# Loading one row of W2 in five few-engine transfers between the K/V loads, and moving the loads of x, gate and biases

## The chip, the cores and the metric

The kernel runs on one core of a Trainium2 chip. The metric is the device time of one execution in microseconds (us), median over runs. Before the change it is 364.52 us over 3 runs (364.5 to 364.59).

## What is computed

A decode step for 8 sequences mixes two branches with a learned gate. Cut to what matters (all tensors bfloat16; B = 8, D = 576, 32 query heads, 16 K/V heads of 128, cache length 8192, window W = 2048, F = 4608):

```python
def reference(A_x, A_k_cache, A_v_cache, A_wq, A_wo, B_x, B_w1, B_b1, B_w2, B_b2, gate_w):
    x = A_x
    g = _sigmoid((x * gate_w).sum(-1, keepdims=True))
    # attention over the last W = 2048 positions of the caches
    q = (x @ wq).reshape(B, Sq, Hq, Dh).transpose(0, 2, 1, 3)
    k = jnp.repeat(k_cache[:, :, Sk - W:, :], rep, axis=1)
    v = jnp.repeat(v_cache[:, :, Sk - W:, :], rep, axis=1)
    p = _softmax(jnp.einsum("bhqd,bhkd->bhqk", q, k) * (Dh ** -0.5))
    o = jnp.einsum("bhqk,bhkd->bhqd", p, v)
    a = o.transpose(0, 2, 1, 3).reshape(B, Sq, Hq * Dh) @ wo
    # two-layer MLP on the normalised input
    y = _layernorm(x)
    h = _gelu(jnp.einsum("bsd,df->bsf", y, w1) + b1)
    b = jnp.einsum("bsf,fd->bsd", h, w2) + b2
    return g * a + (1 - g) * b
```

Almost all of the work is reading: 32 blocks of 4 MB from the two caches and about 20 MB of weights. Each number that is read is used once or a few times.

## The kernel before

**Who issues what.** Every load is issued by SyncE (SP) on one queue; the 16 DMA engines of the core share the transfers of that queue. The kernel is written as a list of operations with dependences (`deps`, which become semaphore waits) and bare order (`after`). A planner (`_Plan.schedule`) with a cost for each operation turns the list into one fixed order per engine. The order on SP is chained by hand: each load has `after=last_dma[-1:]`, so it keeps the order of the text below.

**The first loads (L407 to L417).** In this order: the last 64 rows of Wq (`d_wqr`), the other 512 rows (`d_wqm`, 4 MB), x (`d_x`, 8 rows of 1152 bytes), the gate weights (`d_gw`, one row of 1152 bytes), b1 (`d_b1`, 4 rows of 2304 bytes), b2 (`d_b2`, one row of 1152 bytes), then W1 in two loads (`d_w1m`, 4.5 MB, and `d_w1r`). x starts the prologue: transposes of x on TensorE (L430), the gate (L440 to L458), the layer norm (L446 to L453), q (`o_qp`, L515), the selection of q's heads (`o_selp`, L530), the first MLP product (`o_hp`, L551), GELU and the transpose of h (`o_hT`, L562). b2 enters through a small accumulating product `m2_b` (L856), placed right after `o_hp`.

**The stream (L586 to L618).** 16 units of K and 16 of V follow, 4 MB each, as K0, K1, V0, K2, V1, K3 and so on. Four slots hold them in turn; a load waits on SP until the slot's last reader is done (`slot_free`). For each unit VectorE transposes K (`tr`, L718), TensorE multiplies q by it (`qk`, L732), VectorE takes a maximum (L645), ScalarE the exponential (L649), and TensorE multiplies by V (`pv`, L755 with the helper at L188).

**The end.** W2 has 4608 rows, laid on 128 partitions with 36 rows each, so "column j" is one row for each partition: 128 pieces of 1152 bytes, 41,472 bytes apart in memory. After the last V come 24 columns of W2 (`M` 0), Wo in two loads (`W` 0 and 1), and the last 12 columns of W2 as three loads of 8, 3 and 1 columns (`M` 1), from

```python
        M_CUTS = [[24], [8, 3, 1]]
        stream += [("M", 0), ("W", 0), ("W", 1), ("M", 1)]
```

All their products are added up in one bank of PSUM by `AccGroup` (L570 to L583, matmul at L579). Then VectorE and ScalarE copy one half each (L900 and L901) and SP stores the output (L903).

Of the kernel before, what the change touches and what calls it, by code (L numbers as in the profile page):

```python
# [191 lines left out]
        tile_size=(128, 128), tile_position=(0, 0)))  # L192


def build_kernel(nc, A_x, A_k_cache, A_v_cache, A_wq, A_wo, B_x, B_w1, B_b1, B_w2, B_b2, gate_w, out):
    B, Sq, D = A_x.shape
    _, Hkv, Sk, Dh = A_k_cache.shape
# [27 lines left out]
    with ExitStack() as es:  # L225
# [74 lines left out]
        def aoffs(name):  # L300
            return R[name][0] // 2
# [71 lines left out]
        OC = 64  # L373

        eng_sems = {e: es.enter_context(nc.semaphore("sem_" + e)) for e in ENGS}
        dma_keys = ["x", "g", "b", "b2", "wq", "w1", "out"] + ["s%d" % i for i in range(ND + 1)] + ["t%d" % i for i in range(5)]
        dma_sems = {k: es.enter_context(nc.semaphore("dma_" + k)) for k in dma_keys}

        P = _Plan()
# [28 lines left out]
        d_wqm = dma("sp", lambda e: e.dma_start(wq_m.rearrange("p t c -> p (t c)"), A_wq[0:512, :].rearrange("(p t) c -> p (t c)", t=4)), "wq", 512 * 8192, name="d_wqm", after=[d_wqr])  # L408
        dwq = [d_wqm, d_wqr]
        d_x = dma("sp", lambda e: e.dma_start(x_sb, x2), "x", 8 * D * 2, name="d_x", after=[d_wqm])  # L410
        d_gw = dma("sp", lambda e: e.dma_start(gw_sb, gate_w.partition_broadcast(1)), "g", D * 2, name="d_gw", after=[d_x])
        d_b1 = dma("sp", lambda e: e.dma_start(b1c, B_b1.rearrange("(c f) -> c f", c=FC)), "b", F * 2, name="d_b1", after=[d_gw])
        d_b2 = dma("sp", lambda e: e.dma_start(b2_sb, B_b2.partition_broadcast(1)), "b2", D * 2, name="d_b2", after=[d_b1])
        dx = [d_x]
        db = [d_b1]
        d_w1m = dma("sp", lambda e: e.dma_start(w1_m.rearrange("p t c -> p (t c)"), B_w1[0:512, :].rearrange("(p t) c -> p (t c)", t=4)), "w1", 512 * F * 2, name="d_w1m", after=[d_b2])
        d_w1r = dma("sp", lambda e: e.dma_start(w1_r, B_w1[512:576, :].rearrange("k (s c) -> (k s) c", s=2)), "w1", 64 * F * 2, name="d_w1r", after=[d_w1m])  # L417
        dw1 = [d_w1m, d_w1r]


# [167 lines left out]
        for vi in range(NU):  # L588
# [252 lines left out]
            if i == 0:  # L841
                filler("fill", 8, o_m2[-1:])

        o_m2, o_bias = [], []

        def filler(name, n, after):
            def fn(e):
# [5 lines left out]
            o_m2.append(add("pe", fn, deps=[exp_done[NU - 1], o_mrow, o_mcol], name=name, cost=0.21 * n, after=after))  # L853

        def bias(i):
            o_bias.append(AccGroup("m2_b", [(ob[:, 0:8], b2_sb), (ob[:, 8:16], b2_sb)], [d_b2, o_obl, o_obh], cost=0.6, after=[o_hp]).op)  # L856

        def m2_chunk(ci):
            s = take_slot()
            j = sum(sum(c) for c in M_CUTS[:ci])  # L860
            at = 0
            src = B_w2.rearrange("(p j) n -> p (j n)", j=FT)
            ops = []
            for n, jn in enumerate(M_CUTS[ci]):
                d = dma("sp", (lambda j=j, jn=jn, at=at: lambda e: e.dma_start(slot(s)[:, at * D:(at + jn) * D], src[:, j * D:(j + jn) * D]))(),
                        "t%d" % (sum(len(c) for c in M_CUTS[:ci]) + n), 128 * jn * D * 2, deps=slot_free[s] if n == 0 else [], name="d_w2_%d_%d" % (ci, n), after=last_dma[-1:])
                last_dma.append(d)
                mms = [(hT[:, j + k, 0:8], slot(s)[:, (at + k) * D:(at + k + 1) * D]) for k in range(jn)]
# [4 lines left out]
            slot_free[s] = ops  # L873

        query(0)
# [81 lines left out]
```

## Time and profile before

| what | value |
|---|---|
| median of 3 runs | 364.52 us (364.5 to 364.59) |
| profiled execution, span | 363.0 us |
| what lies around the span (364.52 - 363.0) | 1.5 us |
| mean granted TensorE clock | 0.958 |
| DMA: bytes, mean rate | 154.45 MB, 426 GB/s |
| PE / DVE / ACT / POOL busy | 82% / 64% / 46% / 6% |

The span goes from the first to the last instruction of the core. The busy shares are averages over the whole span. In the answers of the trace "DMA share" is the mean busy share of the 16 DMA engines in a stretch of time; a transfer's packet counts in the stretch in which it starts, so that a stretch shorter than a packet can show more than 1. "us to landing" runs from the issue on SP to the last completion, with the time in the queue.

### The profile page before, as it was taken

How to read it: one execution, taken by the hardware profiler on the slowest of the kernel's cores; microseconds unless marked ns; L12 is line 12 of the kernel's file. 1: busy time of each engine (PE TensorE's matmuls, PEld its weight loads, DVE VectorE, ACT ScalarE, POOL GpSimd, SP SyncE). 2: the span in 40 equal slices, each digit the busy share in tenths (PEclk: the TensorE clock that was granted, in tenths of full speed). 3: DMA queues.
4: the chain of work that ended last, by engine and by line, in shares of the span. 5: the costliest groups of instructions: out<-in, count | busy, mean ns of one | idle time of the engine just before them, and what ended most of it. 6: DMA issues, size and time to landing. Idle time of an engine off the chain costs nothing.

```text
span 363.0 us, 4821 instructions
## 1 busy us (share of the span) xinstructions
PE 297.9 (82%) x1954; PEld 125.3 (35%) x1423; DVE 231.4 (64%) x166; ACT 168.6 (46%) x130; POOL 22.9 (6%) x52
## 2 busy tenths in 40 slices
PE   0456366999999979998897979997989698999875
PEld 0111000434252615242433417150615152436742
DVE  0452989576666694929385768566675949295720
ACT  1022106656647463663637373838374554656000
POOL 9032030000010000000100000000000000003000
PEclk9976598999999998999999989999999999999999
DMA  8999999999999999999999999999999999999996
GB/s 347 436 437 406 455 412 455 412 455 412 450 415 451 415 451 413 441 426 441 426 441 426 435 430 437 430 437 428 437 430 437 430 435 430 437 430 433 415 430 257
DMA packets 6102, 154.45 MB, mean 426 GB/s; under 512 B 694, under 2 KB 840, under 8 KB 1228
## 3 DMA queue, kind: packets, MB, share of 16 engines
q1 hardware_dynamic: 6092, 154.30, 98.8%
q8 instruction: 8, 0.13, 0.1%
q14 instruction: 2, 0.02, 0.0%
HBM read 154.29 MB, written 0.01 MB: 425 GB/s over the span
## 4 chain that ended last, share of the span: by engine, by line
DMA 56%; DVE 27%; PE 14%; issue 1%; ACT 1%; SPq 0%; POOL 0%
DMA arena<-in_A_k_cache_dram 47%; DVE arena L718 21%; PE ps L175 6%; DMA arena<-in_B_w_dram 6%; DMA arena<-in_A_x_dram 3%; DVE arena L668 2%; PE ps L188 2%; PE ps L755 2%; PE ps L732 2%; DVE arena L645 1%; PE ps L501 0%; PE ps L579 0%; DVE arena L557 0%; DVE arena L521 0%; ACT arena L536 0%
## 5 line engine op out<-in xcount | busy, mean ns | idle before, releaser
L718 DVE STREAM_TRANSPOSE arena<-arena 128x4096 f32<-128x4096 f32 (+1 forms) x34 | 141.7, 4175 | 21.9 <-DMA arena<-in_A_k_cache_dram 21.9
L674 ACT ACTIVATE arena<-arena 32x2048 bf16<-32x2048 bf16 x60 | 114.5, 1908 | 71.4 <-DVE arena L668 42.9
L175 PE MATMUL ps<-arena 128*128 128x512 bf16 (+3 forms) x531 | 136.1, 402 | 0.0
L188 PE MATMUL ps<-arena 128*128 x840 | 109.5, 277 | 7.3 <-issue 1.2
L188 PEld LDWEIGHTS ps<-arena 128*128 x840 | 81.4, 97 | 34.3 <-issue 19.0
L732 PE MATMUL ps<-arena 128*128 128x512 bf16 x128 | 51.4, 401 | 27.6 <-DVE arena L718 26.1
L645 DVE TENSOR_REDUCE arena<-ps 128x1 f32<-128x2048 f32 x16 | 36.7, 2291 | 53.8 <-PE ps L175 53.8
L732 PEld LDWEIGHTS ps<-arena 128*128 128x128 bf16 x128 | 12.5, 98 | 131.7 <-issue 75.3
L649 ACT ACTIVATE arena<-ps,arena 128x2048 bf16<-128x2048 f32 x16 | 40.7, 2543 | 0.5
L646 ACT ACTIVATE arena<-arena 128x1 f32<-128x1 f32 x16 | 3.2, 203 | 63.5 <-DVE arena L645 63.5
L755 PE MATMUL ps<-arena 128*128 128x256 bf16 x184 | 25.3, 272 | 1.1 <-DVE arena L663 1.1
L755 PEld LDWEIGHTS ps<-arena 128*128 128x128 bf16 x184 | 16.9, 99 | 18.8 <-issue 14.6
L668 DVE STREAM_TRANSPOSE arena<-arena 128x1024 f32<-128x1024 f32 x15 | 18.1, 1205 | 2.9 <-ACT arena L649 2.9
L579 PE MATMUL ps<-arena 128*8 128x288 bf16 (+1 forms) x140 | 9.6, 286 | 4.0 <-DMA arena<-in_A_wo_dram 3.3
L739 POOL MEMSET arena<- 128x4096 f32 x1 | 3.5, 3511 | 148.2 <-PE ps L175 148.2
L685 PE MATMUL ps<-arena 128*128 128x512 bf16 x16 | 6.5, 407 | 6.5 <-ACT arena L649 5.2
L629 POOL COPY arena<-arena 32x64 bf16<-32x64 bf16 x16 | 3.7, 229 | 123.3 <-PE ps L175 122.4
L901 ACT ACTIVATE arena<-ps 8x288 bf16<-8x288 f32 x1 | 0.4, 402 | 19.5 <-PE ps L579 19.5
L422 DVE COPY arena<-arena 8x128 bf16<-8x128 bf16 x2 | 0.5, 228 | 13.9 <-DMA arena<-in_A_x_dram 13.9
L579 PEld LDWEIGHTS ps<-arena 128*8 128x8 bf16 (+1 forms) x140 | 5.8, 86 | 9.9 <-DMA arena<-in_A_wo_dram 3.3
L900 DVE CAST arena<-ps 8x288 bf16<-8x288 f32 x1 | 0.4, 446 | 12.3 <-PE ps L579 12.3
L557 DVE TENSOR_TENSOR arena<-arena 128x1152 f32<-128x1152 f32 x1 | 1.4, 1358 | 9.7 <-ACT arena L555 9.7
(106 smaller groups left out, 94.0 us busy)
## 6 DMA issues: line engine op xcount, KB each, us to landing
arena<-in_A_k_cache_dram SPq DMA_DIRECT2D x16, 4096.0 KB, 28.7
arena<-in_A_v_cache_dram SPq DMA_DIRECT2D x16, 4096.0 KB, 25.5
arena<-in_B_w_dram SPq DMA_DIRECT2D x1, 4608.0 KB, 22.0
arena<-in_A_wo_dram SPq DMA_DIRECT2D x2, 2304.0 KB, 23.8
arena<-in_A_wq_dram SPq DMA_DIRECT2D x1, 4096.0 KB, 12.6
arena<-in_B_w_dram SPq DMA_DIRECT2D x1, 3456.0 KB, 24.1
arena<-in_B_w_dram SPq DMA_DIRECT2D x1, 1152.0 KB, 22.3
arena<-in_B_w_dram SPq DMA_DIRECT2D x1, 576.0 KB, 23.0
```

Of the source, the lines that this page charges most:

```text
L175: return e.add_instruction(mybir.InstMatmult(name=nc.get_next_instruction_name(), engine=mybir.EngineType.PE, ins=[e.lower_ap(rhs), e.lowe ...
L188: return e.add_instruction(mybir.InstMatmult(name=nc.get_next_instruction_name(), engine=mybir.EngineType.PE, ins=[rhs, lhsT], outs=[e.low ...
L579: ins = e.matmul(ps[32 * j:32 * j + 8, BK_ACC, 0:JN], lhsT, rhs[:, JN * j:JN * j + JN], start=False, stop=True, skip_group_check=True, til ...
L629: return e.tensor_copy(dst, src)
L645: mx = add("dve", lambda e: e.tensor_reduce(out=k(g, MX + x), in_=scores, axis=AXL.X, op=ALU.max), deps=[qk_unit[t]], name="mx%d" % t, cos ...
L649: ex = add("act", lambda e: e.activation(out=bass.AP(arena, offset=aoffs("P"), ap=[[AST, 128], [64, 32], [1, 2], [2, 32]]), in_=ps[:, 0:4, ...
L668: pc = add("dve", lambda e: e.transpose(view("PC").bitcast(F32), view("P").bitcast(F32)), deps=[ex] + (sp_done[t - 1][0] if t else [o_acc0 ...
L674: return e.activation(out=bass.AP(arena, offset=32 * a * AST + aoffs(home) + 64 * a, ap=[[AST, 32], [256, 32], [1, 64]]), in_=bass.AP(aren ...
L685: mm = e.matmul(*args, start=True, stop=False, skip_group_check=True) if n == 0 else held_matmul(nc, e, *args, start=True, stop=False, ski ...
L718: return e.transpose(bass.AP(arena_f, offset=foffs(base) + 2048 * h0, ap=[[AST // 2, 128], [1, 2048 * nh]]), bass.AP(arena_f, offset=foffs ...
L732: mm = e.matmul(*args, start=False, stop=True, skip_group_check=True) if rc == 0 else held_matmul(nc, e, *args, stop=True, skip=True)
L755: return e.matmul(dst, bass.AP(arena, offset=aoffs(home) + 256 * q + ee, ap=[[AST, 128], [2, 128]]), slot(s).rearrange("p (r k d) -> p r k ...
```

## The change

It has three parts.

1. **Order of the first loads.** x comes between the two loads of Wq, the gate weights between Wq and W1, b1 between the two loads of W1, and b2 between K0 and K1. `m2_b` now waits for that later b2.
2. **One column of W2 out of the end.** The last three loads of W2 are 7, 3 and 1 columns instead of 8, 3 and 1. The last column (128 rows of 1152 bytes) goes to a place of its own, `w2x`, which is laid over the constants `sel` and `sel4` once `o_selp` and `o_hp` have read them. A small product `m2_x` uses it.
3. **How that column is read.** Five loads, put into the stream behind K3, K4, K5, K6 and K7, each read as n groups of m rows: 16 x 1, 11 x 3, 5 x 13, 3 x 4 and 2 x 1. The destination has n x m partitions, the source an outer dimension of n. They are built by a new helper that takes both patterns as they are written.

```diff
+def grouped_read(nc, e, dst, src):
+    return e.add_instruction(mybir.InstDMACopy(
+        name=nc.get_next_instruction_name(), engine=mybir.EngineType.SP, queue="qSPDynamicHW", mode="Copy",
+        ins=e.lower_ap_dma(src), outs=e.lower_ap_dma(dst), oob_is_err=True, cce_op=ALU.bypass))
...
-        req("sel", 4 * 128, BF)
-        req("sel4", 128, BF)
+        req("selb", 5 * 128, BF)
...
+        over("sel", "selb", 0, 4 * 128, BF)
+        over("sel4", "selb", 1024, 128, BF)
+        over("w2x", "selb", 0, D, BF)
...
-        d_wqm = dma("sp", ..., name="d_wqm", after=[d_wqr])
+        d_x = dma("sp", ..., name="d_x", after=[d_wqr])
+        d_wqm = dma("sp", ..., name="d_wqm", after=[d_x])
-        d_x = dma("sp", ..., name="d_x", after=[d_wqm])
-        d_gw = dma("sp", ..., name="d_gw", after=[d_x])
-        d_b1 = dma("sp", ..., name="d_b1", after=[d_gw])
-        d_b2 = dma("sp", ..., name="d_b2", after=[d_b1])
+        d_gw = dma("sp", ..., name="d_gw", after=[d_wqm])
+        d_w1m = dma("sp", ..., name="d_w1m", after=[d_gw])
+        d_b1 = dma("sp", ..., name="d_b1", after=[d_w1m])
+        d_w1r = dma("sp", ..., name="d_w1r", after=[d_b1])
-        d_w1m = dma("sp", ..., name="d_w1m", after=[d_b2])
-        d_w1r = dma("sp", ..., name="d_w1r", after=[d_w1m])
...
-        M_CUTS = [[24], [8, 3, 1]]
+        M_CUTS = [[24], [7, 3, 1]]
...
         def m2_chunk(ci):
...
+            if ci == 0:
+                o_m2.append(AccGroup("m2_x", [(hT[:, FT - 1, 0:8], w2x)], [o_hT, d_w2x[-1]], cost=0.2, prio=-1, after=o_m2[-1:]).op)
...
+        w2x = view("w2x")
+        X_PARTS = [(16, 1), (11, 3), (5, 13), (3, 4), (2, 1)]
+        d_w2x = []
+
+        def bias_row(i):
+            d_b2.append(dma("sp", lambda e: e.dma_start(b2_sb, B_b2.partition_broadcast(1)), "b2", D * 2, name="d_b2", after=last_dma[-1:]))
+            last_dma.append(d_b2[0])
+            bias(0)
+
+        def row_part(i):
+            n, m = X_PARTS[i]
+            p0 = sum(a * b for a, b in X_PARTS[:i])
+            dst = bass.AP(arena, offset=p0 * AST + aoffs("w2x"), ap=[[AST, n * m], [1, 1], [1, D]])
+            src = B_w2.rearrange("(p j) n -> p (j n)", j=FT)[p0:p0 + n * m, (FT - 1) * D:FT * D].rearrange("(n m) c -> n m c", n=n)
+            d_w2x.append(dma("sp", lambda e: grouped_read(nc, e, dst, src), "w2x", n * m * D * 2, deps=[o_selp, o_hp] if i == 0 else [], name="d_w2x%d" % i, after=last_dma[-1:]))
+            last_dma.append(d_w2x[-1])
+
+        stream.insert(1, ("B", 0))
+        for i in range(len(X_PARTS)):
+            stream.insert(7 + 3 * i, ("R", i))
...
-        bias(0)
         for kind, i in stream:
-            {"K": k_item, "V": v_item, "W": wo_chunk, "M": m2_chunk, "B": bias}[kind](i)
+            {"K": k_item, "V": v_item, "W": wo_chunk, "M": m2_chunk, "B": bias_row, "R": row_part}[kind](i)
```

When the changed kernel is built, the planner puts `m2_x` on TensorE between the two halves of the QK products of K7; `m2_b` stays right behind `o_hp`; on GpSimd two small copies for the head selection move ahead of eight others. The order of everything else on each engine's long stretch is that of before.

More of the change, by code (lines that the diff above doesn't have):

```diff
@@ L375, in build_kernel @@
         eng_sems = {e: es.enter_context(nc.semaphore("sem_" + e)) for e in ENGS}
-        dma_keys = ["x", "g", "b", "b2", "wq", "w1", "out"] + ["s%d" % i for i in range(ND + 1)] + ["t%d" % i for i in range(5)]
+        dma_keys = ["x", "g", "b", "b2", "wq", "w1", "w2x", "out"] + ["s%d" % i for i in range(ND + 1)] + ["t%d" % i for i in range(5)]
         dma_sems = {k: es.enter_context(nc.semaphore("dma_" + k)) for k in dma_keys}
@@ L407, in build_kernel @@
         d_wqr = dma("sp", lambda e: e.dma_start(wq_r, A_wq[512:576, :].rearrange("k (s c) -> (k s) c", s=2)), "wq", 64 * 8192, name="d_wqr")
[L408 removed]
+        d_x = dma("sp", lambda e: e.dma_start(x_sb, x2), "x", 8 * D * 2, name="d_x", after=[d_wqr])
+        d_wqm = dma("sp", lambda e: e.dma_start(wq_m.rearrange("p t c -> p (t c)"), A_wq[0:512, :].rearrange("(p t) c -> p (t c)", t=4)), "wq", 512 * 8192, name="d_wqm", after=[d_x])
         dwq = [d_wqm, d_wqr]
[L410 to L413, printed above, removed]
+        d_gw = dma("sp", lambda e: e.dma_start(gw_sb, gate_w.partition_broadcast(1)), "g", D * 2, name="d_gw", after=[d_wqm])
+        d_w1m = dma("sp", lambda e: e.dma_start(w1_m.rearrange("p t c -> p (t c)"), B_w1[0:512, :].rearrange("(p t) c -> p (t c)", t=4)), "w1", 512 * F * 2, name="d_w1m", after=[d_gw])
+        d_b1 = dma("sp", lambda e: e.dma_start(b1c, B_b1.rearrange("(c f) -> c f", c=FC)), "b", F * 2, name="d_b1", after=[d_w1m])
+        d_w1r = dma("sp", lambda e: e.dma_start(w1_r, B_w1[512:576, :].rearrange("k (s c) -> (k s) c", s=2)), "w1", 64 * F * 2, name="d_w1r", after=[d_b1])
         dx = [d_x]
         db = [d_b1]
[L416 to L417 removed]
         dw1 = [d_w1m, d_w1r]
@@ L855, in bias @@
         def bias(i):
-            o_bias.append(AccGroup("m2_b", [(ob[:, 0:8], b2_sb), (ob[:, 8:16], b2_sb)], [d_b2, o_obl, o_obh], cost=0.6, after=[o_hp]).op)
+            o_bias.append(AccGroup("m2_b", [(ob[:, 0:8], b2_sb), (ob[:, 8:16], b2_sb)], [d_b2[0], o_obl, o_obh], cost=0.6, after=[o_hp]).op)
         def m2_chunk(ci):
@@ L873, in m2_chunk @@
             slot_free[s] = ops
+        w2x = view("w2x")
[12 more added lines that the diff above has]
+            last_dma.append(d_w2x[-1])
+        assert sum(a * b for a, b in X_PARTS) == 128
+        stream.insert(1, ("B", 0))
+        for i in range(len(X_PARTS)):
+            stream.insert(7 + 3 * i, ("R", i))
         query(0)
-        bias(0)
         for kind, i in stream:
-            {"K": k_item, "V": v_item, "W": wo_chunk, "M": m2_chunk, "B": bias}[kind](i)
+            {"K": k_item, "V": v_item, "W": wo_chunk, "M": m2_chunk, "B": bias_row, "R": row_part}[kind](i)
         seq = []
```

2 lines of the change are left out of this document (1 added, 1 removed).

## The prediction

> **What bounds the kernel now.** I read the page first (DMA line, DMA queues, chain), then the windows of DMA share, then the timeline of the last microseconds. The page:
>
> ```profile
> span 363.0 us, 4821 instructions
> ...
> DMA  8999999999999999999999999999999999999996
> ...
> DMA packets 6102, 154.45 MB, mean 426 GB/s; under 512 B 694, under 2 KB 840, under 8 KB 1228
> ...
> q8 instruction: 8, 0.13, 0.1%
> ...
> DMA 56%; DVE 27%; PE 14%; issue 1%; ACT 1%; SPq 0%; POOL 0%
> ```
>
> The DMA engines are busy in every slice but the first and the last. The chain has DVE and PE pieces too, but the windows say that they only run beside a full queue:
>
> ```profile
> 36.00:100.00 64.00, 50.48 (x260) 15.59 (x162) 50.17 (x18) 30.88 (x22) 3.51 (x1) 0.89 1.00 434
> 100.00:200.00 100.00, 90.88 (x560) 39.12 (x409) 68.45 (x44) 55.72 (x41) 1.84 (x8) 0.98 1.00 432
> 200.00:300.00 100.00, 87.00 (x554) 38.23 (x403) 68.52 (x46) 54.26 (x40) 0.00 (x0) 0.98 1.00 432
> ```
>
> The last two numbers are DMA share and GB/s: share 1.00 and 432 to 434 GB/s from 36 to 300 us, with no hole. So the time is a short start, the bytes at this rate, and what follows the last byte. Each of the 16 engines moves 432 / 16 = 27 bytes per ns. The change moves the same bytes, so it can only alter how evenly the engines end, what small loads cost them, and the start. The end, first by DMA share, then by instructions:
>
> ```profile
> 357.00:358.60 1.60, 1.60 (x30) 1.10 (x24) 0.00 (x0) 0.00 (x0) 0.00 (x0) 1.00 0.97 405
> 358.60:359.00 0.40, 0.17 (x4) 0.00 (x0) 0.00 (x0) 0.00 (x0) 0.00 (x0) 1.00 0.72 279
> 359.00:359.20 0.20, 0.00 (x0) 0.00 (x0) 0.00 (x0) 0.00 (x0) 0.00 (x0) 1.00 0.80 317
> 359.20:359.40 0.20, 0.02 (x2) 0.02 (x4) 0.00 (x0) 0.00 (x0) 0.00 (x0) 1.00 0.59 230
> 359.40:359.60 0.20, 0.20 (x4) 0.16 (x6) 0.00 (x0) 0.00 (x0) 0.00 (x0) 1.00 0.67 271
> 359.60:359.80 0.20, 0.20 (x8) 0.14 (x4) 0.00 (x0) 0.00 (x0) 0.00 (x0) 1.00 0.41 161
> 359.80:360.00 0.20, 0.20 (x8) 0.14 (x5) 0.00 (x0) 0.00 (x0) 0.00 (x0) 1.00 0.53 196
> 360.00:360.20 0.20, 0.20 (x8) 0.17 (x4) 0.00 (x0) 0.00 (x0) 0.00 (x0) 1.00 0.46 161
> 360.20:360.40 0.20, 0.20 (x6) 0.01 (x2) 0.00 (x0) 0.00 (x0) 0.00 (x0) 1.00 0.22 75
> 360.40:360.60 0.20, 0.20 (x8) 0.15 (x6) 0.00 (x0) 0.00 (x0) 0.00 (x0) 1.00 0.00 0
> ```
>
> ```profile
> 360.42 0.22 PEld L579 LDWEIGHTS ps<-arena 128*8 128x8 bf16 x6 [0.21 <-DMA arena<-in_B_w_dram]
> 360.79 0.09 PEld L579 LDWEIGHTS ps<-arena 128*8 128x8 bf16 x2 [0.15 <-DMA arena<-in_B_w_dram]
> 361.12 0.40 ACT L901 ACTIVATE arena<-ps 8x288 bf16<-8x288 f32 x1 [19.48 <-PE ps L579]
> ...
> 361.61 0.32 SPq L903 DMA_DIRECT2D out_dram<-arena  x1
> ```
>
> The engines do not end together. From 358.6 to 360.4 the idle part is 0.4 x 0.28 + 0.2 x (0.20 + 0.41 + 0.33 + 0.59 + 0.47 + 0.54 + 0.78) = 0.11 + 0.66 = 0.78 us per engine. At 360.0 to 360.2 still 0.46 x 16 = 7.4 engines move data, and half of the engines have ended up to 1.5 us before. TensorE waits for the last of them (360.79), and from there to the end stand 363.0 - 360.79 = 2.2 us that the change leaves alone. So 0.78 us, 0.21% of 364.52, is the most that any redistribution of the same bytes can gain.
>
> The q8 line fits a late half: eight code packets, 0.13 MB / 8 = 16 KB each, 0.1% of 16 x 363 us = 5.8 us in all, 0.7 us each (0.4 to 1.1 with the rounding), at the cost of the engine that carries one. The Trainium skill (Runtime: NRT & Kernel Launch, Instruction fetch mechanics) says that crossing a 16 KB block of code is "mostly hidden". The size agrees with this trace, but a full DMA queue hides nothing from the engine that carries the block.
>
> **The first loads.** Pieces of the chain in order of time, then SP's issues in the timeline:
>
> ```profile
> 1.71 12.15 DMA arena<-in_A_x_dram
> ...
> 37.67 4.45 DVE arena L718
> 42.12 0.05 issue
> 42.16 0.61 PE ps L732
> ```
>
> ```profile
> 1.71 0.37 SPq L410 DMA_DIRECT2D arena<-in_A_x_dram  x1
> ...
> 2.40 0.42 SPq L412 DMA_DIRECT2D arena<-in_B_b_dram  x1
> ...
> 3.23 0.36 SPq L416 DMA_DIRECT2D arena<-in_B_w_dram  x1
> ...
> 19.39 0.54 SPq L618 DMA_DIRECT2D arena<-in_A_v_cache_dram  x1
> 33.04 0.54 SPq L618 DMA_DIRECT2D arena<-in_A_k_cache_dram  x1
> ```
>
> x lands at 13.86 (1.71 + 12.15) because it queues behind 4 MB of Wq; in the changed kernel it lands some 10 us earlier, and the norm of the MLP with it, while the gate still waits for Wq. q gets no faster than its own Wq. Nothing of this reaches the end: V0 is issued at 19.39 and K2 at 33.04, and the queue holds 10 MB of weights and two K units, 18 MB, or 42 us at 432 GB/s; even K2 a few us later finds V0 before it. Cost 0; with the cover gone it would be the shift of K2's issue, under 1 us. b1 lands before the W1 rest that its reader needs anyway. b2 now lands behind K0 (about 37.6 us, where the transpose of K0 starts); its four products hold TensorE for 4 x 0.29 us then, ahead of QK products that start at 42.16 in any case. Cost 0, cover over 3 us.
>
> What small loads cost the engines that carry them can be bounded:
>
> ```profile
> arena<-in_B_w_dram SPq DMA_DIRECT2D x1, 4608.0 KB, 22.0
> ...
> L579 PE MATMUL ps<-arena 128*8 128x288 bf16 (+1 forms) x140 | 9.6, 286 | 4.0 <-DMA arena<-in_A_wo_dram 3.3
> ```
>
> W1's 4.72 MB are issued at 3.23 and land at 25.2, 11.4 us behind x; at 432 GB/s they need 10.9. So x, gate, b1 and b2 together cost the worst engine about 0.45 us, 0.11 each with their bytes. Spread between large transfers they cost that or less. That engine need not be one that ends last, so a gain at the end lies between 0 and 0.4 us; I take 0, since a late half of eight engines stays.
>
> **The column moved out of the end.** For each engine 8 of 128 rows, 9216 bytes, go: 9216 / 27 = 0.34 us earlier for all 16. The two last weight loads wait for DMAs that land 0.37 us apart, and the last of these is one column, 8 rows per engine: 0.046 us per row, with the border between two loads in it.
>
> **The column in five loads.** With n groups on n engines, and every load starting at the same engine, the engines get 1+3+13+4+1 = 22 rows (two engines), 21 (one), 17 (two), 4 (six) and 1 (five): 1.01, 0.97, 0.78, 0.18 and 0.05 us. The Trainium skill (DMA: Bandwidth & Descriptors, Why a DMA increments its semaphore by 16 and not by 1) says just this of SP's queue: the number of engines divides the outermost sizes of both sides, and the lowest-numbered ones are used. The trace of before shows no engine's number. If it were otherwise the worst engine would have 13 rows or more.
>
> So net of the 0.34: five engines end later by 0.44 to 0.67 us, six earlier by 0.16, five earlier by 0.29. What counts is whether one of the five loaded engines belongs to the late half. If lateness had nothing to do with the choice, all five would be early in C(8,5)/C(16,5) = 56/4368, 1 of 78. The late ones lie within 0.4 us of the last (360.0 to 360.4), so a loaded late engine ends between 0.44 - 0.4 and 0.67 - 0 after the old end: 0.0 to +0.7, and with two or three of the five late the worst decides: **+0.4 us**.
>
> Per load there may be a gap on top. The lower bound is the border between the last loads, nothing beyond 0.046 per row; the upper one the 0.11 - 0.046 = 0.06 above, 0.3 us for the five on the worst engines. The nearer row is the lower (a small load right behind a large one), so I take 0 and keep 0.3.
>
> The same page (Rules for kernel authors) speaks against the change: use all 16 engines, and coalesce, since under 64 KB one pays "mostly overhead"; its fit of 2.0 us per DMA would give an estimate of 10 us for five loads one after another. The 0.37 us between two landings says that a queued load pays no such sum.
>
> The other steps cost nothing that counts. Five issues of 0.42 us on SP: SP waits far longer (the waits of SP's queue; then one line of TensorE's timeline),
>
> ```profile
> SPq L618 <- PE ps L755: 101.6, 8, 13.6
> ```
>
> ```profile
> 173.15 0.40 PE L732 MATMUL ps<-arena 128*128 128x512 bf16 x1 [1.68 <-DVE arena L718]
> ```
>
> and the loads queue behind issued units. Their first wait (`o_selp`, `o_hp`) is over when K2 is issued. `m2_x`, 2 x 0.29 us, stands ahead of the second half of K7's QK, where TensorE sits idle 1.68 us; the last of the five loads lands about with K7, some 8 us before. If it were late, K7's scores and all of TensorE behind them would wait.
>
> **The sum.** Profiled execution 363.0 + 0.4 = 363.4 us; with the 1.5 us around it 364.52 + 0.4 = **364.9 us**. A measurement of this kernel tells about 0.2%, 0.73 us, from no change, so this is within it.
>
> **Rivals.** (1) *The loaded engines are the early ones.* Then the five fill their idle time (up to 1.5 us of room for at most 1.01), and the end moves by the late engines with 1 or 4 rows: -0.29 to -0.16, **364.3 us**. For it: the room is there, and low-numbered engines may escape the code packets for a reason that no view shows. Against it: 1 of 78 by chance. (2) *Gaps at each small load on the most loaded engine, which is among the last*: 0.67 for its rows and 0.2 to 0.3 for five gaps, +0.9, **365.4 us**, slower by 0.24%. It decides, in that place, once each load costs over 0.02 us beyond its rows. For it: the 0.11 us; against it: the small loads stood next to each other there. (3) *The loads spread over all 16 engines* and are no few-engine loads: 8 rows each, 0.37 - 0.34, **364.5 us**.
>
> **How the numbers follow.** Forecast 0.45, (1) 0.27, (2) 0.15, (3) 0.13. The range 364.1 to 365.6 takes in rival 1 with -0.4 and rival 2 with 0.2 above its value; outside I leave about 0.15. Faster by over 0.2% would need 0.73 of the 0.78 us: 0.05. Slower by over 0.2%: rival 2 and the edge of the forecast, 0.17. Within: 0.78.
>
> **What would show it.** DMA share 1.00 and 432 GB/s up to 300 us as before. At the end the wait of the last L579 weight load ends 0.4 us later than 360.79, with few engines in the last stretch (share near 0.1); in rival 1 it ends earlier and the share falls steeply from near 1; in rival 3 the tail has the old form. x's first copy starts near 4 us. A hole in the DMA share between 15 and 340 us, or an end more than 1 us away, would prove the argument wrong.

## The result, and the profile after

| | before | after |
|---|---|---|
| median of 6 runs | 364.51 us (364.1 to 364.76) | 368.52 us (366.27 to 372.51) |
| profiled execution | 364.5 us, span 363.0 | 369.31 us, span 367.7 |

The changed kernel is 4.0 us slower by the medians. The ratio is 1.0097, 95% interval 1.0074 to 1.012; like every ratio below it leaves out runs that lie over 1.5% above the fastest of their kernel (here 372.51). The forecast was 364.9 with a range up to 365.6. The runs of before lie within 0.7 us, those of after within 6.2: something in the new kernel goes differently from one execution to the next. The profiled execution of after (369.31 us) is its second longest.

The page of after (span, DMA by slices and GB/s, packets, code loading, chain):

```profile
span 367.7 us, 4826 instructions
...
DMA  8999999999999999999999999999999999999994
GB/s 300 439 414 430 446 414 446 424 438 405 397 437 421 411 431 447 419 432 424 446 438 428 430 424 446 435 428 430 428 446 435 428 430 428 442 438 421 425 421 184
DMA packets 6267, 154.45 MB, mean 420 GB/s; under 512 B 731, under 2 KB 1005, under 8 KB 1521
...
q8 instruction: 8, 0.13, 0.1%
...
DMA 63%; DVE 24%; PE 11%; SPq 1%; issue 0%
```

The bytes are the same 154.45 MB and the DMA line still shows no hole: share 9 in every slice between the first and the last. Only the GB/s line tells of a loss, and only weakly. There are 165 packets more: 128 rows and 16 + 11 + 5 + 3 + 2 = 37 completions, one for each engine that a load uses. So the five loads run on as many engines as they were written for, and rival 3 (all 16) is out.

Where the time went is read from windows with equal borders. Both kernels, each line: stretch, length, five engines' busy time, granted clock, DMA share, GB/s. First before:

```profile
2.00:13.00 11.00, 0.45 (x1) 0.13 (x1) 0.00 (x0) 0.08 (x1) 7.97 (x14) 1.00 1.01 426
13.00:36.00 23.00, 14.97 (x133) 3.45 (x70) 10.50 (x25) 4.78 (x11) 4.76 (x20) 0.78 1.02 435
36.00:84.00 48.00, 35.12 (x165) 8.73 (x90) 38.07 (x14) 21.66 (x15) 3.51 (x1) 0.86 1.01 435
84.00:104.00 20.00, 19.30 (x121) 8.55 (x90) 13.93 (x5) 10.77 (x8) 0.92 (x4) 1.00 0.99 426
104.00:124.00 20.00, 19.27 (x124) 9.23 (x95) 13.96 (x12) 12.92 (x10) 0.00 (x0) 1.00 1.02 439
124.00:164.00 40.00, 36.45 (x233) 15.96 (x169) 27.64 (x18) 21.62 (x17) 0.00 (x0) 0.96 1.00 433
```

Then after, with its tail:

```profile
2.00:13.00 11.00, 0.69 (x7) 0.39 (x7) 7.49 (x9) 0.08 (x1) 8.54 (x15) 1.00 1.01 395
13.00:36.00 23.00, 14.89 (x123) 3.38 (x60) 5.43 (x15) 2.84 (x10) 4.26 (x19) 0.78 1.00 427
36.00:84.00 48.00, 32.93 (x156) 8.59 (x91) 39.93 (x15) 20.64 (x16) 3.51 (x1) 0.86 1.00 433
84.00:104.00 20.00, 19.32 (x114) 7.28 (x76) 12.09 (x4) 13.11 (x9) 0.00 (x0) 1.00 1.01 408
104.00:124.00 20.00, 18.85 (x116) 8.07 (x85) 13.43 (x8) 11.19 (x9) 0.92 (x4) 1.00 1.00 430
124.00:164.00 40.00, 34.48 (x225) 15.07 (x161) 28.59 (x22) 21.02 (x15) 0.00 (x0) 1.00 1.01 427
164.00:204.00 40.00, 34.93 (x213) 15.02 (x158) 25.80 (x14) 21.32 (x16) 0.92 (x4) 1.00 1.00 433
...
360.00:362.00 2.00, 0.62 (x9) 0.32 (x10) 0.00 (x0) 0.00 (x0) 0.00 (x0) 1.00 0.88 361
362.00:364.00 2.00, 1.72 (x29) 1.05 (x26) 0.00 (x0) 0.00 (x0) 0.00 (x0) 1.00 0.36 142
364.00:365.60 1.60, 1.49 (x22) 0.81 (x22) 0.00 (x0) 0.00 (x0) 0.00 (x0) 1.00 0.08 30
```

The bytes that after moves less in these stretches, at 432 GB/s: 31 x 11 / 432 = 0.8 us in the stretch with x between the two Wq loads, 0.4 in the next, 0.2 up to 84; then 0.8, 0.4 and 0.6 us in the stretches from 84 to 164, into which the five loads were put. That is 3.2 us, all before 164; from there on the rate is that of before. The rest is at the end: idle 2 x 0.12 + 2 x 0.64 + 1.6 x 0.92 = 3.0 us per engine against 0.78, so 2.2 us more. Together 5.4 us for the 4.7 us of the two spans (a packet counts in the window where it starts, and the packets that lie around each border make up some tenths).

The chain in order of time says the same by the starts of the K transposes on VectorE, which follow the arrival of K units. After, for the units that arrive at about 40, 109, 149, 188 and 304 us:

```profile
40.26 4.46 DVE arena L725
...
109.42 4.45 DVE arena L725
...
148.65 4.45 DVE arena L725
...
187.62 4.45 DVE arena L725
...
303.73 4.45 DVE arena L725
```

And the same of before (its first, 37.67, stands in the prediction):

```profile
105.09 4.45 DVE arena L718
...
143.77 4.45 DVE arena L718
...
182.52 4.45 DVE arena L718
...
298.78 4.45 DVE arena L718
```

The last engine's K unit is 2.6 us late at the first, 4.3, 4.9 and 5.1 us late at the next three, and 4.95 us late at 304: nothing is lost after 188. The end, from the timeline of after:

```profile
365.13 0.22 PEld L586 LDWEIGHTS ps<-arena 128*8 128x8 bf16 x6 [0.43 <-DMA arena<-in_B_w_dram]
365.50 0.09 PEld L586 LDWEIGHTS ps<-arena 128*8 128x8 bf16 x2 [0.15 <-DMA arena<-in_B_w_dram]
...
366.32 0.31 SPq L933 DMA_DIRECT2D out_dram<-arena  x1
```

The last weight load starts at 365.50 against 360.79, and the store 4.71 us later than before as well (366.32 against 361.61): the whole loss lies in the arrival of data.

One thing no view shows is the time of a single packet; it is in the trace. A 32 KB packet of a K or V transfer takes 1213 ns on each engine in the undisturbed stretches of both kernels. Behind the first of the five loads, from 84.5 us on, the packets of after grow over four rounds, and from about 90 to 96 us those of *all 16* engines take 1353 to 1361 ns; the whole 4 MB transfer takes 10.6 us instead of 9.7. They are slower by 12%, without a gap between them. So the DMA share stays at 1.00 while the rate falls. Behind the second to fourth load only one to three packets of an engine are slower (up to 1565 ns). The 32 KB packets of Wq behind x take 1311 ns on average and up to 2025 (before: 1227 and 1358).

### The profile page after: what moved, and what is told of

It reads as the page before. It is cut to its first block, busy times and chain, and to the rows that moved or that the text cites. A ratio compares the mean times of both kernels' runs of the same rounds, so it can differ in the third digit from the quotient of the medians.

```text
span 367.7 us, 4826 instructions
## 1 busy us (share of the span) xinstructions
PE 298.2 (81%) x1954; PEld 125.2 (34%) x1423; DVE 235.8 (64%) x166; ACT 168.5 (46%) x130; POOL 23.0 (6%) x52
## 2 busy tenths in 40 slices
DMA packets 6267, 154.45 MB, mean 420 GB/s; under 512 B 731, under 2 KB 1005, under 8 KB 1521
## 4 chain that ended last, share of the span: by engine, by line
DMA 63%; DVE 24%; PE 11%; SPq 1%; issue 0%
DMA arena<-in_A_k_cache_dram 57%; DVE arena L725 20%; DMA arena<-in_B_w_dram 6%; PE ps L175 5%; DVE arena L675 2%; PE ps L188 2%; PE ps L762 2%; PE ps L739 2%; DVE arena L652 1%; PE ps L586 0%; DVE arena L930 0%; SPq L415 0%; SPq L416 0%; SPq L421 0%; SPq L417 0%
## 6 DMA issues: line engine op xcount, KB each, us to landing
arena<-in_A_wq_dram SPq DMA_DIRECT2D x1, 4096.0 KB, 15.3
```

## The experiments

The theories carry the letters of the expectations; those that came up late are explained there. *Collision* (A): a small load between large transfers costs the stream time beyond its bytes, at x's new place and at the five loads. *Pile-up* (B), the rival: what the prediction had, only the uneven ends of the engines. When B turned out too small, A was split for the five loads: that the *unevenness* of a load does the harm (A1), that *any* small load does it by chance (A2), that *tiny* loads do it (A3), or that it is the *bytes per engine*, whether they fill whole units of 512 bytes (C). Each kernel's time is the median (lowest to highest, number of runs), beside runs of before on the same chip: 364.48 (first group), 364.46, 364.45, 364.53 and 364.45 (the last). All 102 of these runs lie within 364.23 to 364.94, so what is seen beyond that comes with the kernels and not with the chip.

### The parts alone

**e1_order**: only the new order of x, gate, b1 and b2; W2 as before.

```diff
+        d_x = dma("sp", ..., name="d_x", after=[d_wqr])
+        d_wqm = dma("sp", ..., name="d_wqm", after=[d_x])
...
+        d_gw = dma("sp", ..., name="d_gw", after=[d_wqm])
+        d_b1 = dma("sp", ..., name="d_b1", after=[d_w1m])
...
+        stream.insert(1, ("B", 0))
```

> Only the new order of the first loads (x, gate, b1, b2 between large ones); the end of W2 stays 8, 3, 1 columns. Theory A (collision: a small load that many engines carry, queued directly ahead of a large one, leaves the engines reading in a pattern in which all of them run below 432 GB/s for some microseconds, and spreads them): x on eight engines ahead of Wq does this, so DMA from 2 to 13 us is near 390 GB/s instead of 420 to 430 and the time is 1 to 3 us above before. Theory B (pile-up: the time comes from the rows that the loaded engines carry): nothing is piled up here, within 0.3 us of before.

**e2_rows**: only the column in five loads; the first loads as before.

```diff
-        M_CUTS = [[24], [8, 3, 1]]
+        M_CUTS = [[24], [7, 3, 1]]
...
+        X_PARTS = [(16, 1), (11, 3), (5, 13), (3, 4), (2, 1)]
...
+            stream.insert(6 + 3 * i, ("R", i))
```

> Only the column of W2 in five few-engine loads and the end of 7, 3, 1 columns; the first loads stand as before. Theory A: DMA falls to 385 to 420 GB/s in the 10 us behind the first small load (behind K3, near 85 us) and for shorter behind the next ones; +1.5 to +3 us. Theory B: 432 GB/s throughout, one or a few engines end late, +0.4 to +1 us.

**e3_one**: e2_rows with one load of 8 rows on each of the 16 engines behind K3:

```diff
-        X_PARTS = [(16, 1), (11, 3), (5, 13), (3, 4), (2, 1)]
+        X_PARTS = [(16, 8)]
```

> As the five loads alone, but the column comes in one load of 16 groups of 8 rows, all 16 engines alike, behind K3. Theory A: one slow stretch behind K3 as with the first of the five loads, +0.5 to +1.5 us. Theory B: nobody is loaded more than another, within 0.2 us of before.

**e5_nox**: e1_order with x behind the second Wq load; gate, b1 and b2 keep their new places:

```diff
-        d_x = dma("sp", ..., name="d_x", after=[d_wqr])
-        d_wqm = dma("sp", ..., name="d_wqm", after=[d_x])
+        d_wqm = dma("sp", ..., name="d_wqm", after=[d_wqr])
+        d_x = dma("sp", ..., name="d_x", after=[d_wqm])
```

> The new order of the first loads but with x behind Wq as before: only gate, b1 and b2 stand between large loads (one, four and one engine). Theory A: few engines are touched, within 0.3 us of before, and with the order alone 1 to 3 us slower the whole loss of the order is x. Theory B: within 0.3 us; it says nothing of a difference between this and the order alone.

Measured: e1_order 366.27 us (364.6 to 367.26, 6), ratio 1.004 [1.0017, 1.0062]; e2_rows 365.96 (364.83 to 369.72, 10), 1.0073 [1.0034, 1.0111]; e3_one 364.85 (364.55 to 365.13, 10), 1.001 [1.0001, 1.002]; e5_nox 364.48 (364.37 to 364.97, 10), 1.0003 [0.9994, 1.0013].

The order alone costs 1.8 us by the medians (its runs lie between 0.1 and 2.8 us above before), and e5_nox, which differs from it by x's place only, costs nothing. So it is x, 9 KB, between the two Wq loads; gate, b1 and b2 between large transfers are harmless. The end of the profiled e1_order (span 365.6):

```profile
357.00:359.00 2.00, 1.84 (x14) 0.29 (x5) 0.00 (x0) 0.00 (x0) 0.00 (x0) 0.95 0.95 396
359.00:361.00 2.00, 2.00 (x31) 1.20 (x30) 0.00 (x0) 0.00 (x0) 0.00 (x0) 1.00 0.45 176
361.00:363.00 2.00, 1.51 (x26) 0.80 (x20) 0.00 (x0) 0.00 (x0) 0.00 (x0) 1.00 0.06 23
```

At a share of 0.06, 0.06 x 16 = 1 engine moves data alone for 2 us. In the trace one engine ends Wq at 16.2 us, the others between 13.5 and 13.9; in the transfer that ends near 84 us it is the last at 86.5, and nothing levels this out up to the end. The idle part here is 2 x 0.05 + 2 x 0.55 + 2 x 0.94 = 3.1 us per engine, as much as the 3.0 us at the end of after. So x alone brings about an end as uneven as that of after; the profile of e2_rows, without it, has no such end.

The five loads alone have two groups of times: 5 of 10 runs between 364.83 and 365.47, one 366.46, 4 between 368.93 and 369.72. The lower group has the size of the forecast, 0.4 to 1.0 above before. The upper group, 4.4 us higher on average, is what the forecast has no term for; no run of it has a profile.

### Which loads do it

**f1_even5**: e2_rows with the five loads on all 16 engines, as even as they can be.

```diff
-        X_PARTS = [(16, 1), (11, 3), (5, 13), (3, 4), (2, 1)]
+        X_PARTS = [(16, 1), (16, 1), (16, 2), (16, 2), (16, 2)]
```

> As the five loads alone, at the same five places, but each on all 16 engines alike: 16 groups of 1, 1, 2, 2 and 2 rows. Theory A1 (unevenness: a load that only some engines carry shifts these against the others, and shifted engines collide in their reads): nothing is shifted, within 0.3 us of the one even load's 364.85 and as narrow (364.5 to 365.2). Theory A2 (any small load ahead of a large one makes the engines collide): five times the chance, so above 365.5 or with single runs near 369 as with the five uneven loads. Theory B (pile-up of rows): 364.5, since all carry 8 rows.

**f2_8x16**: e2_rows with one load, 16 rows on each of 8 engines.

```diff
-        X_PARTS = [(16, 1), (11, 3), (5, 13), (3, 4), (2, 1)]
+        X_PARTS = [(8, 16)]
```

> The column in one load behind K3 on eight engines, 16 rows each. Theory A1: eight engines fall 0.7 us back at once, collisions follow, 365 to 369 with a wide spread. Theory A2: one load as in the even case, 364.85 and narrow. Theory B: eight loaded engines of which some are late ones: 16 x 0.046 - 0.34 = +0.4, 364.6 to 364.9 and narrow.

**f3_end5**: the five loads of e2_rows after the last V, behind the second Wo load, with only the last W2 loads behind them; `m2_x` moves to the end as well:

```diff
-        for i in range(len(X_PARTS)):
-            stream.insert(6 + 3 * i, ("R", i))
+        stream[-1:-1] = [("R", i) for i in range(len(X_PARTS))]
...
```

> The same five uneven loads, but queued behind the second Wo load, right ahead of the last three loads of W2. Theories A1 and A2: only some 3 us of stream are left in which collisions can cost anything, so +0.2 to +1.0 us and no run near 369. Theory B (the pile-up as predicted): the full +0.4 to +0.7 us, 364.9 to 365.2, with few engines in the last 0.5 us.

**f4_start16**: the kernel before, and between the two Wq loads one load of 16 rows of W2, one for each engine, which nothing uses:

```diff
+        d_dum = dma("sp", lambda e: e.dma_start(view("hT", 16)[:, 0:D], B_w2.rearrange("(p j) n -> p (j n)", j=36)[0:16, 35 * D:36 * D]), "dum", 16 * D * 2, name="d_dum", after=[d_wqr])
...
+        d_wqm = dma("sp", ..., name="d_wqm", after=[d_dum])
```

> The kernel before with one added small load between the two loads of Wq: 16 rows of W2's last column to 16 partitions, one row per engine, whose data is not used; x stays behind Wq. Theory A1: even, so within 0.3 us of before (364.5), where x on eight engines at this place cost 1.8 us. Theory A2: like x at this place, 365.5 to 367 and wide.

Measured: f1_even5 370.9 us (367.62 to 378.07, 6), 1.0204 [1.0184, 1.0225]; f2_8x16 365.36 (365.19 to 365.76, 10), 1.0026 [1.0017, 1.0036]; f3_end5 365.12 (364.65 to 366.29, 10), 1.0021 [1.001, 1.0032]; f4_start16 367.2 (366.93 to 367.64, 4), 1.0074 [1.0057, 1.0091].

Unevenness falls as the cause of the long losses: five perfectly even loads are the worst so far, and the most uneven single load (16 rows on half of the engines) has all its runs within 0.6 us of each other (at +0.9 us, of which 16 x 0.046 - 0.34 = 0.4 would be its rows by the prediction's price). f3_end5 was meant to show the pile-up by itself. With the five loads where no K or V transfer follows, they cost 0.66 us. No run is near 369 any more, but two of the ten (366.25 and 366.29) stand 0.9 us above the other eight, and no profile shows why. The windows and the timeline of the end in a run of 365.11 us:

```profile
357.00:359.00 2.00, 1.72 (x29) 1.26 (x31) 0.00 (x0) 0.00 (x0) 0.00 (x0) 1.00 0.96 391
359.00:361.00 2.00, 1.55 (x24) 0.72 (x18) 0.00 (x0) 0.00 (x0) 0.00 (x0) 1.00 0.58 222
```

```profile
362.21 0.31 SPq L928 DMA_DIRECT2D out_dram<-arena  x1
```

The store is issued 0.60 us later than before (361.61). That is the size of the prediction's term, +0.4 between 0.0 and 0.7, but not its picture. A few late engines would have raised the idle part at the end. It is 2 x 0.04 + 2 x 0.42 = 0.9 us per engine, of which 0.1 lies behind the last data at 360.9; before has 0.8. So the engines end as unevenly as before, only all of them later. The packets say why: the 128 packets of the seven W2 columns behind the five loads take 342 ns on average, against 305 in e2_rows and k4_fix, where no small load stands ahead of them; with 8 on each engine that is 0.3 us. In e2_rows, too (its profiled run, 365.16 us, is of the lower group), the packets of an engine add up to 0.68 us more than before and its last data land 0.65 us later. The rows piled on few engines slowed the packets of all 16; that the loaded engines end last is not seen.

The fastest run of f1_even5 is the one with a profile, and even there nearly all packets of two whole transfers take 1353 to 1360 ns, between the second and the third of the five loads:

```profile
84.00:104.00 20.00, 19.34 (x123) 8.89 (x93) 14.32 (x5) 10.44 (x7) 0.92 (x4) 1.00 0.99 423
104.00:124.00 20.00, 19.08 (x119) 8.74 (x91) 13.57 (x12) 12.94 (x10) 0.00 (x0) 1.00 1.02 390
124.00:164.00 40.00, 32.66 (x212) 13.79 (x148) 26.84 (x17) 19.82 (x16) 0.00 (x0) 1.00 0.99 424
```

**g1_even44** and **g2_even17**: two even loads, behind K3 and K4, of 4 and 4 rows an engine, and of 1 and 7.

```diff
-        X_PARTS = [(16, 1), (11, 3), (5, 13), (3, 4), (2, 1)]
+        X_PARTS = [(16, 4), (16, 4)]
```

```diff
-        X_PARTS = [(16, 1), (11, 3), (5, 13), (3, 4), (2, 1)]
+        X_PARTS = [(16, 1), (16, 7)]
```

> The column in two even loads of 16 groups of 4 rows, behind K3 and K4. Theory A3 (tiny: a load that gives an engine only one to three rows, queued between large loads, sets off a stretch in which every 32 KB packet takes some 1360 ns instead of 1213; a load with many rows per engine sets off only a short one): 364.8 to 365.2 and narrow. Theory A2 (any small load ahead of a large one): two chances, 365 to 368 and wide.

> The same two places, but even loads of 1 and 7 rows per engine. Theory A3: the first one sets off the slow stretch, which lasts until the second load or longer, +1 to +3 us, 365.5 to 368 and wide. Theory A2: like the two loads of 4 rows.

**h1_start128** and **f5_start8**: f4_start16 with 8 rows on each of 16 engines, and with 8 rows on 8 engines, one each.

```diff
-        d_dum = dma("sp", lambda e: e.dma_start(view("hT", 16)[:, 0:D], ...[0:16, 35 * D:36 * D]), ...)
+        d_dum = dma("sp", lambda e: e.dma_start(view("hT", 128)[:, 0:D], ...[0:128, 35 * D:36 * D]), ...)
```

```diff
-        d_dum = dma("sp", lambda e: e.dma_start(view("hT", 16)[:, 0:D], ...[0:16, 35 * D:36 * D]), ...)
+        d_dum = dma("sp", lambda e: e.dma_start(view("hT", 8)[:, 0:D], ...[0:8, 35 * D:36 * D]), ...)
```

> The unused load between the two loads of Wq, with 8 rows per engine (128 partitions) instead of one (+2.7 us). Theory A3: many rows per engine, so only their own 0.37 us and a short disturbance, 364.8 to 365.5. Theory A2: as with one row or worse, 367 to 368.

> The unused load between the two loads of Wq with one row on each of eight engines, read from W2 at 41 KB steps; x, which lies in one piece, cost 1.8 us at this place. Theories A2 and A3: the source does not matter, 365 to 367.5, between nothing and the 2.7 us of 16 engines. If the source mattered (rows far apart), more than the 2.7 us per engine's share; if the even 16 were the worse case because all engines are hit at once, below 1.8.

Measured: g1_even44 364.8 us (364.62 to 365.19, 10), 1.0009 [1.0, 1.0019]; g2_even17 381.05 (366.25 to 392.32, 4: 373.34, 388.76, 366.25, 392.32), no useful interval; h1_start128 366.86 (365.58 to 367.75, 4), 1.0072 [1.0055, 1.0089]; f5_start8 366.85 (366.61 to 367.38, 4), 1.0068 [1.0051, 1.0085].

At the start, size and form decide little: any load between the two Wq loads cost 1.8 to 2.7 us by the medians (x, 16 single rows, 8 rows an engine, 8 engines with one row). In the stream form decides: 4 + 4 rows cost 0.35 us, 1 + 7 lose up to 28 us. The profiled run of g2_even17 (373.34 us) shows where:

```profile
84.00:104.00 20.00, 19.25 (x120) 8.39 (x88) 13.69 (x5) 10.99 (x8) 0.92 (x4) 1.00 1.00 398
104.00:124.00 20.00, 18.28 (x114) 8.16 (x86) 13.93 (x12) 11.37 (x10) 0.00 (x0) 1.00 1.02 373
124.00:164.00 40.00, 30.79 (x189) 12.38 (x133) 24.80 (x17) 18.84 (x14) 0.00 (x0) 0.96 0.99 380
164.00:204.00 40.00, 34.25 (x204) 14.17 (x148) 24.83 (x11) 21.49 (x15) 0.92 (x4) 1.00 1.01 434
```

The rate stays low long after the 7-row load behind K4, with no small load near, and then comes back by itself; the packets take 1409 ns here, which is slower than in after. It is a mode that the stream falls into, not a price for each load; and 7 rows an engine are not tiny, so the tiny-load theory falls as well.

### Bytes per engine

One row is 1152 bytes, 2.25 x 512. Four, eight and sixteen rows are whole multiples of 512, one, two, six and seven are not; in the stream, the loads without long runs up to here have the first kind, the others the second. Still open were that rule, and whether a version with such loads beats the kernel before.

**k1_even26**: g1_even44 with 2 and 6 rows.

```diff
-        X_PARTS = [(16, 4), (16, 4)]
+        X_PARTS = [(16, 2), (16, 6)]
```

> Two even loads behind K3 and K4 of 2 and 6 rows per engine. So far 8, 4+4 and 16 rows per engine kept the time within 1 us, and 1+7 and 1+1+2+2+2 cost up to 28 us. Theory C (bytes: a load whose bytes per engine are no multiple of 512 sets off the slow stretches; 2304 and 6912 are none, 4608, 9216 and 18432 are): several us above before and wide, like 1+7. Theory D (count: packets per engine not a multiple of 4): the same. Theory E (only an odd number of rows does it): as 4+4, 364.8.

**k2_d512** and **k3_d640**: the kernel before with eight loads behind K3 to K10, each 16 rows of 512 bytes (or 640) of W2, one an engine, which nothing uses:

```diff
+        def dummy(i):
+            dst = bass.AP(arena, offset=16 * i * AST + aoffs("xT"), ap=[[AST, 16], [1, 256]])
+            src = B_w2.rearrange("(p j) n -> p (j n)", j=FT)[16 * i:16 * i + 16, 0:256]
...
+        for i in range(8):
+            stream.insert(6 + 3 * i, ("Z", i))
```

> The kernel before with eight added loads of 16 rows of 512 bytes, one row per engine, behind K3 to K10, whose data is not used. Theory C: 512 bytes leave no remainder, within 0.5 us of before and narrow. Theories D and E, and any theory by which one short packet per engine is enough: many us above before and wide.

> The same eight unused loads with 640 bytes per row. Theory C: a remainder of 128 as with the 1152 bytes of one row, so several to 30 us above before and wide. Theories D and E: like the 512 bytes.

**k4_fix**: the changed kernel with x back behind both Wq loads and the column in two loads of multiples of 512.

```diff
-        d_x = dma("sp", ..., name="d_x", after=[d_wqr])
-        d_wqm = dma("sp", ..., name="d_wqm", after=[d_x])
+        d_wqm = dma("sp", ..., name="d_wqm", after=[d_wqr])
+        d_x = dma("sp", ..., name="d_x", after=[d_wqm])
...
-        X_PARTS = [(16, 1), (11, 3), (5, 13), (3, 4), (2, 1)]
+        X_PARTS = [(16, 4), (4, 16)]
```

> The change with its triggers taken out: x behind Wq, gate, b1 and b2 between large loads, the column in two loads of 16 groups of 4 and 4 groups of 16 rows behind K3 and K4 (20 rows on four engines, 4 on the others). Theories C, D and E: no slow stretch, and what is left is the pile-up: four engines 20 x 0.046 - 0.34 = +0.58 against late engines -0.16, so 364.3 to 365.1 and narrow.

Measured: k1_even26 365.05 us (364.7 to 382.25, 12; three runs over 381, one 366.6), the ratio without the three 1.0011 [1.0, 1.0021]; k2_d512 364.8 (364.55 to 365.14, 10), 1.0007 [0.9998, 1.0017]; k3_d640 364.94 (364.42 to 367.06, 10, two over 366.8), 1.0021 [1.0004, 1.0038]; k4_fix 365.19 (364.99 to 371.18, 10, one over 365.4), 1.0019 [1.0009, 1.0029].

The profile of k1_even26 caught one of its long runs (381.53 us). GB/s by slices of 9.5 us, then windows:

```profile
DMA  8999999999999999999999999999999999999996
GB/s 331 459 433 429 400 438 442 442 445 429 405 388 386 386 386 385 387 386 386 386 390 386 385 386 386 386 390 416 431 421 435 442 442 436 421 431 424 434 422 265
```

```profile
84.00:104.00 20.00, 19.32 (x119) 8.25 (x86) 13.28 (x5) 11.34 (x8) 0.93 (x4) 1.00 1.02 434
104.00:124.00 20.00, 19.27 (x122) 9.20 (x94) 14.61 (x12) 12.19 (x10) 0.00 (x0) 1.00 0.99 380
124.00:164.00 40.00, 33.38 (x202) 12.89 (x138) 25.55 (x17) 19.54 (x14) 0.00 (x0) 0.96 1.00 387
...
284.00:324.00 40.00, 34.59 (x224) 14.73 (x157) 29.14 (x22) 22.54 (x18) 0.00 (x0) 1.00 1.00 433
```

This is the clearest picture of the mode: 386 GB/s instead of 432 from the second small load at 104 us to about 262 us, flat, with the DMA share at 1.00 all the time; then the old rate. In the trace the packets take 1359 ns again, and 15 transfers take 10.84 us instead of 9.68, 17.4 us in all; the run was 17.0 us over before. The first small load, behind K3, did nothing in this execution.

How often runs fell into the mode, for the kernels with parts of the column or unused rows between K and V transfers. The count goes by times: the mode itself is seen in the profiles of after, f1_even5, g2_even17 and k1_even26 alone. A run counts if it stands more than 0.9 us above its kernel's tight group, or, in the two kernels that have none, because all of their runs stand above 366.2:

| bytes per engine | kernels | runs in the mode |
|---|---|---|
| multiples of 512 in all loads | e3_one, f2_8x16, g1_even44, k2_d512, k4_fix | 1 of 50 (k4_fix, 371.18) |
| others among them | f1_even5 | 6 of 6 |
| | g2_even17 | 4 of 4 |
| | e2_rows | 5 of 10 |
| | k1_even26 | 4 of 12 |
| | k3_d640 (8 loads of 640 bytes) | 2 of 10, mild |

Theory E (an odd number of rows) falls with k1_even26. Theories D (a number of packets per engine that is no multiple of four) and E, and every theory by which one short packet per engine is enough, had k2_d512 many us slower and wide, and it is neither. Theory C had k3_d640 several us slower, and its median is not. What is left of C is a tendency and not a law: 0 of 10 against 2 of 10 runs for k2_d512 and k3_d640 tells little by itself, one run of k4_fix broke the rule, and at the start of the kernel h1_start128 with its multiples of 512 lost as much as the others. e5_nox isn't in the table: its b2, one row of 1152 bytes on one engine between K0 and K1, hurt none of 10 runs. What happens physically in the mode, and why it ends, stays open.

k4_fix takes away most of the loss but does not beat the kernel before: 0.66 us are left. Its profile (365.10 us) shows that they aren't the pile-up either. Behind the load of 16 rows on four engines (at 103 us) the packets of *all 16* engines take 1425 to 1684 ns in one round and up to 1488 in the next, and then 1213 again. That is 0.48 us for each engine, in one transfer. The same short disturbance costs 0.36 us behind the 16 rows on eight engines of f2_8x16 and 0.33 behind the 13 rows on five of e2_rows, but only 0.1 behind the even loads of e3_one and g1_even44 (one profile each). So the mode seems to follow the bytes per engine, and this smaller price the rows that are piled on few engines.

### x at the head

**p1_xfirst**: the kernel before with x ahead of both Wq loads.

```diff
+        d_x = dma("sp", ..., name="d_x")
-        d_wqr = dma("sp", ..., name="d_wqr")
+        d_wqr = dma("sp", ..., name="d_wqr", after=[d_x])
...
-        d_x = dma("sp", ..., name="d_x", after=[d_wqm])
```

> The kernel before with x at the head of the queue, ahead of both loads of Wq; all else as before. If a small load costs at the start because it separates a running load from the 4 MB of Wq behind it (1.8 us for x, 2.4 to 2.7 us for the unused rows), x at the head costs nothing: 364.4 to 364.8 and narrow. If anything small at the start does it, 365.5 to 367. No version here is expected to beat before by more than 0.1 us, since x is not what the end waits for.

Measured: 364.92 us (364.79 to 365.32, 10), 1.0014 [1.0004, 1.0023]. With nothing of size ahead of it x costs 0.47 us and not 1.8, and what it brings (the norm done early) is worth nothing at the end. No version that was run beats the kernel before; e5_nox equals it.

## Why the prediction was wrong

The sign of the likeliest case was right; the size was off by 3.6 us. Point by point:

- **What bounds the kernel: right.** The rate and the unevenness of the engines' ends carry the whole result: 3.2 us and 2.2 us.
- **The inference from it was the first failed step.** "The change moves the same bytes, so it can only alter how evenly the engines end, what small loads cost them, and the start" held the right list, but the rate was then taken as fixed at 432. It can fall to 386 (373 in g2_even17) behind a small load and stay there. The sign named for "right" was half blind too: of "DMA share 1.00 and 432 GB/s up to 300 us" the share stayed, only the GB/s fell.
- **"Spread between large transfers they cost that or less": wrong, and it decided the case.** It bounded the cost of a small load at 0.11 us from x, gate, b1 and b2 of before, which follow one another behind one large transfer. No row of before shows a small load between the K and V transfers, so that bound was none. In its place: nothing measurable for b2 and gate at their new places (e5_nox), 0.4 us for an even 8-row load (e3_one, at the edge of what is told apart), and some 4.4 us more in the upper group of e2_rows, where by its times the mode is hit. Rival 2 had the right place and sign, but 0.06 us a load.
- **x, "Nothing of this reaches the end" and "Cost 0": wrong.** The argument looked at who waits for x and for K2 (rightly: no one). It did not ask what x does to the transfer it was put in front of. e1_order against e5_nox: 1.8 us. The 4 MB Wq load takes 15.3 us from issue to landing in after and 12.6 in before, by their rows of DMA issues.
- **The column, "+0.4 us" between 0.0 and 0.7: right in size, by luck.** f3_end5 and k4_fix both have 0.66 us, and the number of engines of each load is as written (37 completions). But the term was made of loaded engines that end late while the others end early. The traces of f3_end5, e2_rows and k4_fix show ends no less even than before, and packets of all 16 engines that are slower right behind the rows. Rival 1 (the loaded engines are the early ones) missed the time of f3_end5 (364.3 against 365.12). Whether its premise holds stays open, since no view gives an engine's number.
- **The rule of the Trainium skill** (DMA: Bandwidth & Descriptors, Rules for kernel authors) against small loads was set aside because its fit of 2.0 us per DMA is not paid here; and rightly so far as the fit goes: the page gives it for loads that GpSimd issues, these are issued by SP, and eight extra loads in k2_d512 cost 0.3 us, not 16. But its advice to coalesce pointed the right way, for a reason that it does not give: what suffers is not the small load, it is the large ones behind it. Its advice to use all 16 engines did not help by itself (f1_even5, five loads on all 16, +6.4 us).
- **SP, `m2_x`, b2's products: right at 0**, in so far as e5_nox (with the new place of b2 and its products) is at +0.0 and e3_one (with `m2_x`) at +0.4 of data time; none of them was tried alone.

The sum from the parts: 1.8 (x), 0.66 (the short disturbances), and the mode. In the lower group of e2_rows the mode is nearly absent, in the upper one it costs some 4.4 us. That makes 2.5 to 6.9 us against the measured 1.8 to 8.0 of after's six runs. How x's late engine and the slower packets of the five loads add up was not tried beyond after itself.

## What to carry to other kernels

In a kernel bound by one full DMA stream, a small load is not priced by its bytes or its own duration, but by what it does to the large transfers behind it; a bound from small loads in another place does not hold. Look at GB/s by stretches, not at the DMA share, and at single packets' times where the rate falls; and take many runs, since a profile shows one execution of a kernel with two kinds. If a short load has to go between large ones, whole multiples of 512 bytes for each engine did far less harm here (1 of 50 runs), and no version was faster than before, where they stand together right behind the first large transfers.

## What the runs showed of the hardware

- A stream of 4 MB loads can fall into a slower rate: 32 KB packets of about 1360 ns instead of 1213 on all 16 engines, 386 GB/s instead of 432 (after, f1_even5, k1_even26), or of 1409 ns and 373 GB/s (g2_even17). In these four profiles it began right behind a small load, in some executions and not in others, and lasted from about one transfer (after) to 15 (k1_even26) before it ended by itself.
- Many rows on few engines slowed the next one or two 32 KB packets of all 16 engines: to 1425 to 1684 ns in the first round in k4_fix, 0.48 us per engine in all.
- Between the first two loads of the kernel any small load, of 8 to 128 rows, cost 1.8 to 2.7 us by the medians; the same x ahead of both cost 0.47.
- An engine that is made late early stays late: e1_order's was some 2.5 us late after Wq, as late near 84 us, and ran alone at the end.
- Each of the eight code packets (q8) takes 0.9 to 1.0 us in before, within the 0.4 to 1.1 us that the prediction read from the queue's line, and a 32 KB packet beside it takes up to 1.76 us instead of 1.21. So it delays its engine by about 1.4 us. They come at the same places in every kernel (the first at 32 to 36 us, the last at 350 to 367).
